# Other PSUM banks for the second tile's sequence product and the first pair, and matrix blocks and a transposition moved, in a four-layer attention and Fourier kernel

## The chip, the core and the metric

The kernel runs on one core of a Trainium2 chip. The metric is the device time of one execution in microseconds (us); lower is better. Five engines work from instruction queues of their own: TensorE (PE) multiplies matrices, VectorE (DVE), ScalarE (ACT) and GpSimd (POOL) do elementwise work, SyncE (SP) issues nearly all of the DMA transfers. PE writes its products to PSUM, which the kernel uses as eight banks of 128 x 512 fp32.

## The reference

Four sublayers follow each other, A, B, A, B, each with a residual around it, on x of 2048 rows by 640 columns:

```python
x = x + A(layernorm(x))      # layer 0;  layer 2 again, with the same weights
x = x + B(layernorm(x))      # layer 1;  layer 3 again

def A(x, wqkv, wo):          # 32 heads of 20; 8 keys per row at distances 0, 2, ..., 14
    q, k, v = split_heads(x @ wqkv)
    kg, vg = k[idx], v[idx]                    # idx = pos - 2 * arange(8), masked below 0
    attn = softmax(einsum("hsd,hswd->hsw", q, kg) * 20 ** -0.5)
    return einsum("hsw,hswd->hsd", attn, vg) @ wo

def B(x, Cr, Ci, Wr, Wi):    # real part of a two-dimensional Fourier transform
    a, b = x @ Wr.T, x @ Wi.T
    return Cr @ a - Ci @ b
```

Cr and Ci are 2048 x 2048, Wr and Wi 640 x 640, and they come as inputs, as do wqkv and wo.

## The kernel before

**Numbers.** Every fp32 operand of a product is split into a hi and a lo part in the type fp32r, and each product runs as three passes (hi by hi, hi by lo, lo by hi). A split is two instructions: ACT copies the hi part, and DVE (sometimes POOL) subtracts it to get the lo part. Both stand ahead of every product.

**Rows.** The 2048 rows are held in 4 chunks c of 4 blocks j of 128 rows, in a permuted order (even rows first), so that the dilated window becomes a plain one.

**Layer A** (`layer_a`, L242) is one plan written by hand. `at(step, phase, fn)` (L264) puts a function under a step, from -7 to 66, and a phase; at the end all steps are run through, and in each the phases in the order of the list PHASES (L827). All five engines keep exactly that order (`manual_schedule`, L831). In a step stand the product for q, k and v (`qkv_mm`, L352, into banks m0 and m1), the attention itself on DVE and POOL (`qk_mul` L428 with L431 and L433, `soft`, `soft_exp` with L447 and L460, `av_mul` L467 with L469 and then L484 to L486 on POOL), the transpositions (`pc_pe`, L327; L331 is ACT's copy of one), the product with wo (`wo_mm`, L509) and its addition to x (`wo_add`, L159), and the loads: L417 loads a window of k and v.

**Layer B** (`LayerB`, L865) has eight column tiles t of 256 output columns of the sequence transform, Cr and Ci side by side in 512 columns. Its work is in three parts:

- *z[0]*, the sequence product of tile 0: 16 steps s, each with the five 128-column pieces k of the normalised x against one block of cs (the matrix of Cr and Ci), 15 matmuls a step, added up in five banks. It is computed within the plan of the layer A before it, one third of a step at a time (table ZTHIRDS), by `z_mm` (L944, matmul L955). The blocks come in two ways. In layer 0, `c_load` loads the raw block to a buffer stg, `c_hi` (L915) and `c_lo` (L942) split it. In layer 2, `c_get` (L933) loads a block that was stored split in the DRAM buffer c0b. Into which of the buffers s0, s2, s3 a block goes is said by `c_tag` (L903), and s0 is also used by the last transpositions of the attention before `wo_mm`.
- *the first two tiles* (`run`, L1266): the five banks of z[0] are evacuated to SBUF as hi and lo (`evac`; the hi copies on ACT, the lo on DVE in L1012 and L1015), the matrices of the hidden transform are loaded and split (`load_w`; ACT L126, DVE L128 and L130; five blocks of wre and five of wim), then the 16 steps of z[1] follow (`zpart`), with the output product of tile 0's first half (`ymm`, matmul L1033, read out with L1046 of `yout`) after step 3 and the first 2 of 5 blocks of its second half after step 13. Beside them DVE, ACT and SP make 20 combinations of x for the pairs (`x_whole` L1078; `x_combine`: L1086, L1087, L1088 and the store L1089, through a ring of two stg buffers). At the end the rest of the output product and the evacuation of z[1].
- *the pairs* (`pair`, L1130): six tiles in three pairs, each with seven products m1 to m7 in Strassen's manner instead of eight. A pair first computes m5, m4 and m7 together in a loop of eight steps i, in two banks each (`product`, L1122). Raw blocks of cs come through `s_raw` (L1105) into buffers win (five) or xa (two), combinations of them are made by L1151, splits by ACT L1115 and DVE L1116, combinations of x are loaded by L1095.

The pair that ends layer 1 is called from `early` (L573) of layer 2 and runs with hooks: at some of its places, the first chunk of layer 2's x is normalised and transposed (`xt(j, part)`: the PE transposition L225 into the bank pq, ACT's L232 and DVE's L236).

**What sets the order.** In layer B only PE keeps the written order (`manual_schedule` of the tensor engine alone, in `run` and `pair`). The order on DVE, ACT, POOL and SP is chosen by the framework's scheduler when the program is built; on the chip each engine then works its list in order. A PSUM bank can be taken by a new product when the last reader of the old one is done. The banks before, in the places around the change:

```python
ZTAGS = ("m0", "m1", "xt", "t0", "t1")                                                   # z[0] and z[1]
            self.ym = [pt([P, 512], f"aux{e}") for e in range(2)]                            # ymm
                m5, m4, m7 = banks("m0", "m1"), banks("xt", "t0"), banks("t1", "pq")           # every pair
```

Of the kernel before, what the change touches and what calls it, by code (L numbers as in the profile page):

```python
# [26 lines left out]
P = 128  # L27
NC = 4
NJ = 4
# [23 lines left out]
STG = (-1, "dma2")  # L53
NWIN = 5
ZTAGS = ("m0", "m1", "xt", "t0", "t1")
NT = 8
NP = 8
NPAIR = 3
# [16 lines left out]
def tile_layers(ctx: ExitStack, tc: tile.TileContext, x, wqkv, wo, cs, wre, wim, out):  # L75
# [10 lines left out]
    def nm(base):  # L86
        uid[0] += 1
        return f"{base}_{uid[0]}"
# [4 lines left out]
    def pt(shape, tag, bufs=1):  # L93
        return ps.tile(shape, F32, tag=tag, name=nm(tag), bufs=bufs)
# [117 lines left out]
    def a_weights_q(q):  # L212
        wt = T([P, 2, KD, 3 * F], f"r1_{q}", F32R)
        for k in range(KD):
            split(wt[:, 0, k], wt[:, 1, k], wq_load1(q, k))
        return wt
# [25 lines left out]
    def layer_a(li, stats, handoff, prev):  # L242
# [21 lines left out]
        def at(step, phase, fn, *args):  # L264
            plan.setdefault((step, phase), []).append((fn, args))
# [5 lines left out]
        def x_load(c, j, tag="xa"):  # L271
            xnT[(c, j)] = load_x(xin[c], j, tag)
# [9 lines left out]
        def x_norm(c, j, fast=False):  # L282
            stats[c].apply(j, xnT[(c, j)], fast)

        def xt_pe(c, j, part, bank):
            if part == 0:
                xnT[(c, j, 1)] = T([P, 2, KD, P], f"s{j}", F32R)
            xnT[(c, j, "p", part)] = t_pe(xnT[(c, j)], part, bank)

        def xt_hi(c, j, part):  # L290
            t_hi(xnT[(c, j, 1)], part, xnT[(c, j, "p", part)])

        def xt_lo(c, j, part):
            t_lo(xnT[(c, j, 1)], part, xnT[(c, j, "p", part)])
# [278 lines left out]
        def early():  # L573
            def x_get(j):
                x_load(0, j)
                x_norm(0, j)

            def w0():
                with tc.issue_after(prev.dma.ins):
                    wq[0] = a_weights_q(0)  # L580

            def xt(j, part):
                xt_pe(0, j, part, "pq")
                xt_hi(0, j, part)
                xt_lo(0, j, part)

            prev.pair(
                NPAIR - 1,
                stats,
                {  # L590
                    2: lambda: (x_get(0), x_get(1)),
                    4: lambda: xt(0, 0),
                    5: lambda: (xt(0, 1), x_get(2)),
                    6: lambda: xt(1, 0),
                    7: lambda: (w0(), xt(1, 1), x_get(3)),
                    ("y", 1): lambda: xt(2, 0),
                    ("y", 2): lambda: xt(2, 1),
                    "end": lambda: (xt(3, 0), xt(3, 1)),
                },
            )  # L600
            for q in range(1, NQ):
                wq[q] = a_weights_q(q)
# [63 lines left out]
        if not first:  # L666
            early()
        pq = pt([P, 512], "pq")
# [47 lines left out]
        for u in range(NG):  # L716
# [9 lines left out]
            for jp in range(2):  # L726
                s = 2 * u + jp
# [21 lines left out]
        for c in range(2):  # L749
# [10 lines left out]
            for j in range(NJ):  # L760
                t = LNS[ly][c] + (2 - c) * j
# [35 lines left out]
        if prev is not None:  # L797
            for j2 in range(2):
                at(j2 - 3, "pe3", prev.ymm, NT - 1, j2, 0, KD)
                at(j2 - 2, "actl", prev.yout, NT - 1, j2, stats)  # L800
        last = 66
# [6 lines left out]
        for z in range(len(thirds) // 3):  # L808
            t = thirds[3 * z]
            if first and z in PRE:  # L810
                at(max(thirds[3 * z - 7] + 1, t - 3), "dmac", handoff.c_get, z)
            elif first:
                at(t - 2, "dmac", handoff.c_load, z)
                at(t - 1, "hi", handoff.c_hi, z)
                at(t - 1, "misc", handoff.c_lo, z, z < NJ)
            else:
                at(t - 1, "dmac", handoff.c_get, z)
            for p in range(3):
                at(thirds[3 * z + p], "pe3", handoff.z_mm, z, p)
        if first:  # L820
# [44 lines left out]
    class LayerB:  # L865
# [35 lines left out]
            nc.vector.tensor_scalar(self.xl[(c, j)], xr[(c, j)], nmean, rstd, op0=ALU.add, op1=ALU.mult)  # L901

        def c_tag(self, s, t=0):  # L903
            tags = ("s3", "s0", "s2") if self.li == 1 else ("s0", "s2", "s3")
            if t:
                return (tags[0], tags[-1 if self.li == 3 else 1])[s % 2]
            return tags[s % 3] if s < NST - 1 else "s1"

        def c_load(self, s, t=0):
# [33 lines left out]

        def z_mm(self, s, p, t=0):  # L944
            if s == 0 and p in (None, 0):
                self.z[t] = [pt([P, 512], tag) for tag in ZTAGS]
            c, j = divmod(s, NJ)
            order = [(i, k) for i in range(3) for k in range(KD)]
            if s in (0, NST - 1):
                order = [(i, k) for k in range(KD) for i in range(3)]  # L950
            if p is not None:
                order = order[5 * p : 5 * p + 5]
            for i, k in order:
                a, b = PASSES[i]
                self.last = nc.tensor.matmul(  # L955
                    self.z[t][k],
                    self.xn[c][:, a, j, k * P : (k + 1) * P],
                    self.ct[s][:, b],
                    start=s == 0 and i == 0,
                    stop=s == NST - 1 and i == 2,  # L960
                )
# [60 lines left out]
        def ymm(self, t, j2, k0, k1, emajor=False, ks=tuple(range(KD))):  # L1022
            zt = self.zt[t]
            if k0 == 0:
                self.ym = [pt([P, 512], f"aux{e}") for e in range(2)]
            order = [(k, e) for k in ks[k0:k1] for e in range(2)]
            if emajor:
                order.sort(key=lambda ke: ke[1])
            for k, e in order:
                for a, b in PASSES:  # L1030
                    for ri in range(2):
                        w = self.wr[:, b, k] if ri == 0 else self.wi[k][b]
                        self.last = nc.tensor.matmul(  # L1033
                            self.ym[e][:, :320],
                            zt[(k, a, ri)][:, j2 * P : (j2 + 1) * P],
                            w[:, e * 320 : (e + 1) * 320],
                            start=(k, a, b, ri) == (ks[0], 0, 0, 0),
                            stop=(k, a, b, ri) == (ks[-1], 1, 0, 1),
                        )
# [90 lines left out]
        def pair(self, p, nstats, hooks=None):  # L1130
            t1, t2 = 2 * p + 2, 2 * p + 3
# [4 lines left out]
            tags = wide  # L1136
# [30 lines left out]
            def banks(*tg):  # L1167
                return [pt([P, 512], x) for x in tg]
# [3 lines left out]
                    hooks[at]()  # L1172

            with tc.manual_schedule(engines={nc.tensor.engine}):
                m5, m4, m7 = banks("m0", "m1"), banks("xt", "t0"), banks("t1", "pq")
                for i in range(NP):
                    ends = i == 0, i == NP - 1
                    b22, b21, b11 = raw(t2, NP + i), raw(t1, NP + i), raw(t1, i)
# [17 lines left out]
                m1, m2 = banks("m0", "m1"), banks("xt", "t0")  # L1196
# [33 lines left out]
                for i in range(NP):  # L1230
                    ends = i == 0, i == NP - 1
                    if hooks is not None and i == 3:
                        tags = narrow
# [58 lines left out]
    st0 = [None] * NC  # L1292
    b1, b2 = LayerB(1), LayerB(3)
    layer_a(0, st0, b1, None)
    st2 = [None] * NC
    b1.run(st2)
    layer_a(2, st2, b2, b1)
    b2.run(None)
    b2.ytile(NT - 1, 0, None)
    b2.y_final(NT - 1)  # L1300

# [54 lines left out]
```

## Time and profile before

| | |
|---|---|
| timed, median of 3 runs | 1798.74 us (1796.4 to 1799.93) |
| the profiled execution | 1789.91 us |
| its span, first to last instruction | 1788.0 us |
| mean granted clock of PE | 0.994 |
| PE busy in L1033 (output products) | 226.4 us with r2a, 208.2 us with pr |
| PE busy in L362 (q, k, v) | 436.5 us |
| DVE in L1151, win<-win,win | 75.7 us busy, 45.7 us idle just before, most of it waiting for DMA |
| DMA | 425.15 MB, 238 GB/s in the mean |

The profile is one execution. Times in it are us from the span's start. "Busy" is the share of the span in which an engine has an instruction running; "idle before" is the time that it stood just ahead of an instruction, with the work that released it. A group's line names the line of the program, engine, operation, and out<-in buffers by their names without numbers. The layers follow each other in the span: layer 0 to about 380 us, layer 1's own part to about 870, layer 2 to about 1265, then layer 3. Layer 1 and layer 3 run the same code.

### The profile page before, as it was taken

To read this page: it belongs to the slowest core of one execution; us is meant where nothing else is said; L and a number is where in the kernel's file an instruction comes from. 1 tells how busy PE (TensorE), PEld (TensorE's weight loads), DVE (VectorE), ACT (ScalarE), POOL (GpSimd) and SP (SyncE) were. 2 spreads that over 40 slices of the span, in tenths; PEclk is the share of its full clock that TensorE was granted. 3 is DMA by queue.
4 is the path that set the end of the run, shared out by engine and by line. 5 is a ranking of instruction groups with operands and counts; after the bars stand their busy time and mean duration, and the time that the engine had idled before them with its cause. 6 is when DMAs were issued, how large, how long until landed. Compare 5 with 4: busy or idle time off the path is not lost.

```text
span 1788.0 us, 26460 instructions
## 1 busy us (share of the span) xinstructions
PE 1741.6 (97%) x8798; PEld 1507.1 (84%) x8798; DVE 1381.9 (77%) x2139; ACT 813.1 (45%) x1690; POOL 634.8 (36%) x593
## 2 busy tenths in 40 slices
PE   9999998989999999999999999999999999999999
PEld 7889887778888888888888889878787888888888
DVE  6999998887767767767738999989777677677673
ACT  4664544454445445445623344444534443443441
POOL 4899999940000000000017998889300000000000
PEclk9999999999999999999999999999999999999999
DMA  7896678758778687777737866687687766876761
GB/s 248 286 313 211 203 210 269 252 183 282 268 255 264 239 274 252 240 267 249 225 125 224 265 213 218 208 293 248 228 295 259 261 223 224 267 230 228 253 208 52
DMA packets 271849, 425.15 MB, mean 238 GB/s; under 512 B 22592, under 2 KB 150592, under 8 KB 271456
## 3 DMA queue, kind: packets, MB, share of 16 engines
q1 hardware_dynamic: 268512, 421.49, 71.6%
q10 hardware_dynamic: 3200, 1.97, 0.4%
q8 instruction: 70, 1.15, 0.3%
q14 instruction: 67, 0.55, 0.1%
HBM read 338.23 MB, written 85.14 MB: 237 GB/s over the span
## 4 chain that ended last, share of the span: by engine, by line
PE 62%; DVE 14%; POOL 12%; DMA 7%; issue 3%; ACT 2%; SPq 0%; DVEq 0%; ACTq 0%; POOLq 0%
PE aux L1033 13%; PE m L362 12%; PE m L1122 9%; PE t L1122 9%; PE pq L1122 5%; PE xt L1122 5%; POOL pr L484 4%; DVE pr L431 3%; POOL pr L433 3%; DMA win<-cs_in 2%; DVE pr L469 2%; POOL pr L485 2%; PE m L955 2%; PE aux L509 2%; PE t L955 2%
## 5 line engine op out<-in xcount | busy, mean ns | idle before, releaser
L362 PE MATMUL m<-r,s 128*128 128x480 f32 x1920 | 436.5, 382 | 2.1 <-ACT s L232 1.6
L362 PEld LDWEIGHTS m<-r,s 128*128 128x128 f32 x1920 | 355.2, 188 | 55.8 <-ACT s L232 2.6
L1115 ACT CAST r<-win 128x512 fp32r<-128x512 f32 x248 | 151.1, 620 | 172.6 <-DVE win L1151 81.1
L174 POOL TENSOR_TENSOR stats<-stats,mhalf 128x1 f32<-128x1 f32 (+1 forms) x40 | 29.8, 746 | 558.4 <-ACT stats L170 549.1
L1033 PE MATMUL aux<-r2a,zo 128*128 128x320 f32 x768 | 226.4, 309 | 0.0
L484 POOL TENSOR_TENSOR pr<-pr 128x640 f32<-128x640 f32 x126 | 205.9, 1634 | 33.8 <-DVE pr L469 33.2
L1033 PE MATMUL aux<-pr,zo 128*128 128x320 f32 x704 | 208.2, 308 | 0.0
L431 DVE TENSOR_TENSOR pr<-pq,win 128x1280 f32<-128x1280 f32 x128 | 189.8, 1483 | 16.4 <-ACT pq L404 12.3
L1116 DVE TENSOR_TENSOR r<-win,r 128x512 fp32r<-128x512 f32 x248 | 167.4, 688 | 45.0 <-ACT r L1115 43.5
L469 DVE TENSOR_TENSOR pr<-pq,win 128x1280 f32<-128x1280 f32 x128 | 190.9, 1491 | 4.3
L433 POOL TENSOR_TENSOR pr<-pr 128x640 f32<-128x640 f32 x128 | 183.3, 1432 | 16.5 <-DVE pr L431 16.3
L1122 PE MATMUL m<-r,r 128*128 128x512 f32 x606 | 156.4, 392 | 0.8 <-DVE r L1116 0.8
L1033 PEld LDWEIGHTS aux<-r2a,zo 128*128 128x128 f32 x768 | 144.1, 188 | 2.0
L1122 PEld LDWEIGHTS m<-r,r 128*128 128x128 f32 x606 | 113.5, 188 | 26.6 <-DVE r L1116 1.5
L1033 PEld LDWEIGHTS aux<-pr,zo 128*128 128x128 f32 x704 | 132.2, 188 | 2.1
L955 PE MATMUL m<-s,r 128*128 128x512 f32 x384 | 120.1, 400 | 13.4 <-POOL s L942 4.9
L1122 PE MATMUL t<-r,r 128*128 128x512 f32 x483 | 130.7, 393 | 2.0 <-issue 1.2
L955 PE MATMUL t<-s,r 128*128 128x512 f32 x384 | 119.1, 398 | 2.3 <-DVE ot L1015 1.5
L439 DVE TENSOR_REDUCE lg<-pr 128x64 f32<-128x640 f32 x128 | 103.9, 812 | 18.2 <-POOL pr L433 17.8
L485 POOL TENSOR_TENSOR pr<-pr 128x320 f32<-128x320 f32 x126 | 113.0, 897 | 9.9
L1151 DVE TENSOR_TENSOR win<-win,win 128x512 f32<-128x512 f32 x110 | 75.7, 690 | 45.7 <-DMA win<-cs_in 43.9
L1122 PEld LDWEIGHTS t<-r,r 128*128 128x128 f32 x483 | 90.5, 188 | 23.4 <-issue 1.6
(285 smaller groups left out, 3227.8 us busy)
## 6 DMA issues: line engine op xcount, KB each, us to landing
win<-cs_in SPq DMA_DIRECT2D x354, 256.0 KB, 4.2
r<-xc SPq DMA_DIRECT2D x240, 256.0 KB, 4.4
win<-kvb SPq DMA_DIRECT2D x96, 440.0 KB, 4.3
xa<-cs_in SPq DMA_DIRECT2D x122, 256.0 KB, 4.2
win<-kvb SPq DMA_DIRECT2D x64, 360.0 KB, 5.3
xc<-stg SPq DMA_DIRECT2D x40, 512.0 KB, 3.4
kvb<-stg SPq DMA_DIRECT2D x60, 320.0 KB, 4.7
xr<-xs SPq DMA_DIRECT2D x41, 320.0 KB, 3.6
```

What stands on the lines that cost most here:

```text
L362: nc.tensor.matmul(mt[g][:, : 3 * F], st[:, a, k], wq[q][:, b, k], start=n == 0, stop=n == 14)
L431: nc.vector.tensor_tensor(pr, q, wview(u, jp, 0, [[1, FE]]), op=ALU.mult)
L433: nc.gpsimd.tensor_tensor(pv[:, :, 0:10], pv[:, :, 0:10], pv[:, :, 10:20], op=ALU.add)
L439: nc.vector.tensor_reduce(lgs[u][:, 2 * jp : 2 * jp + 2].rearrange("p j w h -> p (j w h)"), prq.pop((u, jp))[:, :, 0:10], axis=AX.X, op=AL ...
L469: nc.vector.tensor_tensor(pr.rearrange("p j w (h d) -> p j w h d", d=DH), lgs[u][:, 2 * jp : 2 * jp + 2].unsqueeze(4).to_broadcast([P, 2, ...
L484: g.tensor_tensor(pr[:, :, 0:4], pr[:, :, 0:4], pr[:, :, 4:8], op=ALU.add)
L485: g.tensor_tensor(pr[:, :, 0:2], pr[:, :, 0:2], pr[:, :, 2:4], op=ALU.add)
L955: self.last = nc.tensor.matmul(self.z[t][k], self.xn[c][:, a, j, k * P : (k + 1) * P], self.ct[s][:, b], start=s == 0 and i == 0, stop=s = ...
L1033: self.last = nc.tensor.matmul(self.ym[e][:, :320], zt[(k, a, ri)][:, j2 * P : (j2 + 1) * P], w[:, e * 320 : (e + 1) * 320], start=(k, a, ...
L1115: nc.scalar.copy(hi, raw)
L1116: nc.vector.tensor_tensor(lo, raw, hi.bitcast(F32), op=ALU.subtract)
L1122: nc.tensor.matmul(bank, w(a, kb), hl[b], start=start and (a, b) == (0, 0), stop=stop and (a, b) == (1, 0),)
```

## The change

Six edits, with the same matmuls before and after:

- z[1] takes the banks aux0, aux1, pq, m0 and m1 (ZTAGS1); z[0] keeps its own.
- The two output products of tile 0 take the banks xt and t0; all others keep aux0 and aux1.
- The first pair's m5, m4 and m7 take t1 and pq, m0 and m1, xt and t0; the other pairs keep theirs.
- In layer 0's plan the lo parts of cs blocks 11 and 12 are computed on POOL and not on DVE.
- In layer 2's plan blocks 0 and 1 are loaded one step earlier (steps 48 and 49 instead of 49 and 50; block 2 stays at 50), and the buffers of layer 3's z[0] go round in the order s2, s0, s3 instead of s0, s2, s3. (The rewritten line for t=1 gives the same buffers as before.)
- In the pair with hooks, the last two transpositions come after blocks k=3 and k=4 of the output product, and not both at its end.

```diff
+ZTAGS1 = ("aux0", "aux1", "pq", "m0", "m1")
...
-                    "end": lambda: (xt(3, 0), xt(3, 1)),
+                    ("y", 3): lambda: xt(3, 0),
+                    ("y", 4): lambda: xt(3, 1),
...
-                at(t - 1, "misc", handoff.c_lo, z, z < NJ)
+                at(t - 1, "misc", handoff.c_lo, z, z < NJ or z in (11, 12))
             else:
-                at(t - 1, "dmac", handoff.c_get, z)
+                at(min(t - 1, 48 + z) if z < 3 else t - 1, "dmac", handoff.c_get, z)
...
         def c_tag(self, s, t=0):
-            tags = ("s3", "s0", "s2") if self.li == 1 else ("s0", "s2", "s3")
             if t:
-                return (tags[0], tags[-1 if self.li == 3 else 1])[s % 2]
+                return (("s3", "s0") if self.li == 1 else ("s0", "s3"))[s % 2]
+            tags = ("s3", "s0", "s2") if self.li == 1 else ("s2", "s0", "s3")
             return tags[s % 3] if s < NST - 1 else "s1"
...
-                self.z[t] = [pt([P, 512], tag) for tag in ZTAGS]
+                self.z[t] = [pt([P, 512], tag) for tag in (ZTAGS, ZTAGS1)[t]]
...
-                self.ym = [pt([P, 512], f"aux{e}") for e in range(2)]
+                self.ym = [pt([P, 512], tag) for tag in (("aux0", "aux1") if t else ("xt", "t0"))]
...
-                m5, m4, m7 = banks("m0", "m1"), banks("xt", "t0"), banks("t1", "pq")
+                if p == 0:
+                    m5, m4, m7 = banks("t1", "pq"), banks("m0", "m1"), banks("xt", "t0")
+                else:
+                    m5, m4, m7 = banks("m0", "m1"), banks("xt", "t0"), banks("t1", "pq")
```

When the changed program is built, the number of instructions of each engine stays, but for two that go from DVE to POOL. The scheduler's order changes at some places of layers 1 and 3. On PE the first three matmuls of m5 stand inside z[1]'s steps 12 and 13. On DVE, some of the splits L942 stand ahead of the L1088 that they were behind, and around the evacuation of z[1] the end of the list is, by lines:

```text
before: L1015 zo, L1046, L1046, L1015 ot, L1151 win<-xa, L1012 ot
after:  L1015 zo, L1151 win<-xa, L1046, L1046, L1015 ot, L1012 ot
```

In layer 2, SP's load of block 0 stands behind the store of L523 and ahead of two window loads; the load of block 1 stands where that of block 0 stood.

## The prediction

> **What bounds the kernel now.** I read the page first, then the waits of TensorE (PE), then its timeline around each place that the change touches, then the other engines' timelines there.
>
> ```profile
> span 1788.0 us, 26460 instructions
> PE 1741.6 (97%) x8798; PEld 1507.1 (84%) x8798; DVE 1381.9 (77%) x2139; ACT 813.1 (45%) x1690; POOL 634.8 (36%) x593
> PE 62%; DVE 14%; POOL 12%; DMA 7%; issue 3%; ACT 2%; SPq 0%; DVEq 0%; ACTq 0%; POOLq 0%
> ```
>
> PE is busy for 97% of the span, and no edit takes a matmul away. So a gain can only be a PE wait that goes, and a loss one that comes. A wait is counted if nothing later absorbs it: in the pairs PE runs through, so a delay there moves the end one to one; inside the attention layers PE waits for the other engines anyway.
>
> Waiting costs twice. Granted clock by window (start:end, length, busy us of PE, PEld, DVE, ACT, POOL with counts, clock, DMA share, GB/s):
>
> ```profile
> 356.50:360.00 3.50, 3.44 (x13) 3.44 (x14) 3.50 (x6) 0.11 (x1) 2.96 (x3) 0.53 0.67 200
> 1176.00:1182.00 6.00, 5.53 (x13) 4.37 (x14) 5.03 (x8) 1.58 (x6) 5.84 (x6) 0.50 1.01 319
> ```
>
> Each follows a wait of 2.10 and 2.07 us. The clock falls to half behind waits of about 2 us, on a grid of 3.41 us (half-clock stretches begin at 264.2, 295.0, 301.8, 356.4 and 1175.6). The same 30 matmuls of L509 took 6.12 us at 356.56 and 4.66 at 1243.54: one fall cost 1.46 us.
>
> **First edit: the banks (layers 1 and 3).** Before, the second tile's sequence product waits for the evacuation of the first tile's last banks. In layer 1 the trace has .24, .76 and .40 us at 401.04, 403.43 and 404.76; with the restart of the pipeline 1.89 us, in layer 3 1.96. With aux0, aux1, pq, m0 and m1 this goes. But the first output product (L1033) follows after four steps, and its k=4 terms need wim's fifth block:
>
> ```profile
> 422.70 0.83 DVE L128 SCALAR_TENSOR_TENSOR zo<-xa,zo 128x640 fp32r<-128x640 f32 x1 [1.01 <-ACT zo L126]
> ```
>
> That ends at 423.53 and PE reaches its terms at 423.58 already, so 1.0 of the 1.9 is lost again; .9 stays.
>
> What decides is the next place, the start of the first pair. There PE waits today for bank t1, freed by the last evacuation, L1012 (start, us, engine, line, operation, tiles, idle before and its releaser):
>
> ```profile
> 473.94 0.38 SPq L1105 DMA_DIRECT2D xa<-cs_in  x1
> ...
> 475.04 0.88 DVE L1046 TENSOR_TENSOR xr<-aux,xr 128x320 f32<-128x320 f32 x2
> 475.84 0.41 DVE L1015 TENSOR_TENSOR ot<-t,zo 128x256 fp32r<-128x256 f32 x1
> 477.57 0.69 DVE L1151 TENSOR_TENSOR win<-xa,win 128x512 f32<-128x512 f32 x1 [1.32 <-DMA xa<-cs_in]
> 478.18 0.68 DVE L1012 TENSOR_TENSOR ot<-t,ot 128x512 fp32r<-128x512 f32 x1
> ...
> 478.96 0.94 PE L1122 MATMUL t<-r,r 128*128 128x512 f32 x3 [0.80 <-PE t L1122]
> ```
>
> DVE works in program order: L1012 was behind L1151, which waited for a load of cs_in. PE had m5 and m4 (12 matmuls) to do meanwhile, and only m7 stood. The instruction order of the changed program puts L1151 further forward, ahead of both L1046 and of the L1015 for ot; and m4, not m7, now takes the banks that these free (m0 holds k=3, m1 k=4). From the landing at 477.57: L1151 .69, two L1046 .88, L1015 .41 with small overlaps end at 479.45, L1012 at 480.1. m4's three matmuls on m0 start at about 479.6, those on m1 at 480.3, and m7 at 481.1 instead of 478.96: **+2.1 us**. The load hangs on the 20 combinations (L1086 to L1089) ahead on DVE and its ring of two buffers, not on PE, so the .9 won before only lengthens this wait. Layer 3 has the same order:
>
> ```profile
> 1364.14 0.69 DVE L1151 TENSOR_TENSOR win<-xa,win 128x512 f32<-128x512 f32 x1 [0.94 <-DMA xa<-cs_in]
> ...
> 1365.53 0.94 PE L1122 MATMUL t<-r,r 128*128 128x512 f32 x3 [1.16 <-issue]
> ```
>
> By the same sum m0 is free at 1366.0 and m7 starts at 1367.5: **+2.0**. Bounds for each: 1.5 and 4, since the load's landing isn't fixed (L1088 now follows L1086 at once and stands for ACT, .7 us; the same kind of load takes 3.0 us at 1361.16 and 3.6 at 473.94).
>
> PE then stands from about 475.6 to 479.6, and from 1362.0 to 1366.1: 4 us each. By the rows above the clock falls behind each: 1.46 and, as part of the window may lie in the wait, 1.4 taken, **+2.8** for both (0 to 2 × 1.7, half of a 3.41 us window). [...]
>
> Other effects of the banks: the first output product's banks xt and t0 are read out by 512 at the latest, and the next product that wants them starts behind 518: nothing.
>
> **Second edit: the lo parts of blocks 11 and 12 move to POOL (end of layer 0).**
>
> ```profile
> 356.83 1.44 DVE L942 TENSOR_TENSOR s<-stg,s 128x512 fp32r<-128x512 f32 x1
> ...
> 364.22 1.28 DVE L942 TENSOR_TENSOR s<-stg,s 128x512 fp32r<-128x512 f32 x1
> 281.60 1.27 POOL L942 TENSOR_TENSOR s<-stg,s 128x512 fp32r<-128x512 f32 x1
> ```
>
> DVE loses 1.44 and 1.28, POOL gains about 1.27 twice (bounds .68, DVE's undisturbed row, and 1.94, POOL's slowest there) against 4.1 us of its idle between 354 and 382. The first removal is hidden: DVE waits for a load of x at 363.39 anyway. The second moves DVE's last product, which ends the layer at 382.2 with POOL's at 382.06. POOL's L174 comes .75 later and so PE's wait at 371.34, which the later ending hides. **−1.2** (0 to −1.8). The waits at 356.56 and the fall of the clock there stay: block 10 is still DVE's.
>
> **Third edit: matrix blocks 0 and 1 in layer 2.** Order and tags change together.
>
> ```profile
> 1166.47 0.92 SPq L417 DMA_DIRECT2D win<-kvb  x2
> 1173.10 0.32 SPq L933 DMA_DIRECT2D s<-c0b  x1
> 1177.32 1.97 SPq L933 DMA_DIRECT2D s<-c0b  x2
> ...
> 1176.47 2.92 PE L955 MATMUL m<-s,r 128*128 128x512 f32 x6 [2.07 <-DMA s<-c0b]
> ...
> 1190.71 0.37 ACT L331 CAST ot<-aux 128x256 fp32r<-128x256 f32 x1 [8.37 <-PE aux L327]
> ```
>
> Block 0's load stands on SP until its buffer s0 is free (1173.10), and the two behind it come at 1177.32, landing after 6.75. Block 0 now uses s2, free at about 1165, ahead of the two window loads: issued near 1166.5, it lands by 1173.2 even at 6.75 us. PE is ready at 1174.4. Block 1 issues at 1173.1 and lands 3.3 to 6.75 later, against 1177.9 when PE wants it. So the 2.07, the half clock and the 1.19 at 1184.12 go, and PE's transposition L327 comes 3.7 to 5.2 earlier. ACT (8.37) waits for it with an exponential behind, and so DVE's 1.51 at 1192.14. But what ends the layer is the attention's last product, at POOL 1266.69; POOL has 4.46 us idle between 1190 and 1202, hardly any after it to 1232, and the next window load limits DVE with 3.53 at 1189.14 while the DMA queues stand at a share of 1.0. I take **−2.5** between 0 and −4.5.
>
> **Fourth edit: the last transposition (start of layer 2).** PE waited 1.04 and .57 for ACT:
>
> ```profile
> 899.20 0.70 PE L362 MATMUL m<-r,s 128*128 128x480 f32 x2 [1.04 <-ACT s L232]
> ```
>
> With xt(3,0) and xt(3,1) between output products the first wait goes, 1.2 with its restart; some .3 may come back on bank pq, which the second part now wants sooner. **−.9** (−.3 to −1.9).
>
> **Sum.** −1.2 − .9 − 2.5 + 2.1 + 2.0 + 2.8 = +2.3. The profiled execution took 1789.91 (span 1788.0 and 1.91 around), so it would take 1792.2. The median of the timed runs is 1798.74, 8.8 above the profiled one; the difference carried over gives **1801.0**. A measurement of this kernel can tell about 0.2%, 3.6 us, from no change: "same" is 1795.1 to 1802.3.
>
> **Rivals.**
> Faster: the cs_in load that L1151 waits for lands earlier, because splits moved past the combinations fill DVE's idle and close the chain sooner. Each us takes one off both waits. From 1.5 us on (a PE wait of 2.5) the clock may hold too: +2.3 − 3.0 − 2.8 = −3.5, at 2 us −4.5, 1794.2; at 3.6 us both waits vanish, with today's .80 and 1.16 as well, and the z product's .9 is kept: 1790. For it: DVE idles .7 several times in the chain for ACT. Against: the chain's last steps follow DMA (L1086 waits for xc<-stg). Layer 2 paying in full (−4.5) would help this side. Chance .25.
> Slower: layer 2 pays nothing, since POOL's saturated stretch sets its end whatever PE does at 1184 (+2.5), and the load lands .7 later in both layers behind the delayed L1088 (+1.4): 1804.9; with full half-clock windows 1805.5. For it: POOL is busy 29.16 of 30 us in 1202 to 1232. Point of decision: whether POOL's 4.46 idle at 1190 shrinks. Chance .28.
> [...] Chance .10.
> Forecast: .37, own range 1798 to 1804, of it .25 within 0.2% and .12 above.
> That the change doesn't do what it says is excluded for the order: the new program's listing shows each move.
>
> **Chances.** Faster .25 + .02 = .27; same .25 + .08 = .33; slower .28 + .12 = .40. The range reaches from the partly earlier load with layer 2 in full (1792) to the slower rival with both loads 1.5 later (1807).
>
> **What would show it.** Right: DVE with an idle ahead of L1151 near 476 and behind it L1046, L1015, L1012; a PE wait of some 4 us just ahead of m4 and a clock near half behind it, in layers 1 and 3; no PE wait on ot tiles near 401 and 1286; SP's c0b load behind 1166; PE's L327 near 1185; PE's wait at 899 gone. Wrong: the pairs start without a wait above 2 us, or L1151 finds its data; POOL's idle at 1190 unchanged with the layer's end unmoved; a new wait of PE on pq near 898.

## The result, and the profile after

The changed kernel took 1801.13 us in the median (22 runs, 1795.26 to 1805.89), the kernel before, run beside it, 1796.3 (22 runs, 1790.2 to 1800.64). The ratio is 1.0028, with a 95% interval of 1.0018 to 1.0037: about 5 us slower. The prediction said +2.3 us and 1801.0; that the figure nearly meets the measured one is partly luck, since the kernel before came out at 1796.3 in 22 runs where it had 1798.74 in 3.

From here on, lines are those of the changed kernel where a fence is of it: L1124 is the pairs' product (L1122 before), L1153 the combination of raw blocks (L1151), L1014 and L1017 the evacuations (L1012, L1015), L1048 the read-out of the output product (L1046), L127 the hi copy (L126).

The page of the changed kernel, from its first lines:

```profile
span 1800.3 us, 26446 instructions
PE 1745.3 (97%) x8798; PEld 1511.1 (84%) x8798; DVE 1382.0 (77%) x2137; ACT 812.1 (45%) x1690; POOL 636.7 (35%) x595
...
PE 57%; DVE 16%; POOL 11%; DMA 9%; issue 3%; ACT 2%; SPq 0%; ACTq 0%; DVEq 0%; POOLq 0%
```

Busy times are within 2 us of those before, but for PE's and the weight loads', which are about 4 us longer: nine windows of 3.41 us at half clock lie in this span, six in the one before. On the chain, DVE and DMA have gained what PE lost. The two spans, 1788.0 and 1800.3, must not be subtracted: the first execution was among the quickest (1789.91, below all 22 timed ones), and a second profile of the kernel before took 1796.04.

PE's waits in the changed kernel, around the first two tiles of layer 1 (line, what it waited for: us in total, times, longest):

```profile
PE m L1124 <- DVE ot L1017: 2.8, 1, 2.8
PE xt L1035 <- ACT zo L127: 2.3, 1, 2.3
...
PE xt L1035 <- DVE zo L129: 0.7, 1, 0.7
```

and of layer 3:

```profile
PE xt L1035 <- ACT zo L127: 2.9, 1, 2.9
PE m L1124 <- DVE ot L1017: 2.5, 1, 2.5
```

The waits of z[1] for L1015 and L1012 are gone. In their place stand one in the first output product (L1035, at its k=4 terms, for the two parts of wim's fifth block) and one ahead of m4 (L1124). DVE and PE around the second, in the changed kernel:

```profile
474.56 0.42 DVE L1017 TENSOR_TENSOR zo<-m,zo 128x256 fp32r<-128x256 f32 x1
476.77 0.69 DVE L1153 TENSOR_TENSOR win<-xa,win 128x512 f32<-128x512 f32 x1 [1.79 <-DMA xa<-cs_in]
477.38 0.48 DVE L1048 TENSOR_TENSOR xr<-xt,xr 128x320 f32<-128x320 f32 x1
477.78 0.48 DVE L1048 TENSOR_TENSOR xr<-t,xr 128x320 f32<-128x320 f32 x1
478.18 0.42 DVE L1017 TENSOR_TENSOR ot<-m,zo 128x256 fp32r<-128x256 f32 x1
478.51 0.68 DVE L1014 TENSOR_TENSOR ot<-m,ot 128x512 fp32r<-128x512 f32 x1
...
478.74 2.90 PE L1124 MATMUL m<-r 128*128 128x512 f32 x6 [2.80 <-DVE ot L1017]
481.44 1.18 PE L1124 MATMUL xt<-r,r 128*128 128x512 f32 x3
```

This shows the queue: L1153 stands 1.79 us for its load, and behind it, in order, the read-outs and the L1017 that frees m0. m4 starts 0.14 us after that L1017 ends, and its six matmuls take 2.90 us where six in a row take 1.56 (m7 in the run e6 below). Why so long is shown by the windows of 3.41 us (start:end, length, busy us of PE, PEld, DVE, ACT, POOL, clock, DMA share, GB/s):

```profile
475.30:478.72 3.42, 0.64 (x3) 0.20 (x2) 1.95 (x5) 1.61 (x3) 0.00 (x0) 1.00 0.38 125
478.72:482.13 3.41, 3.39 (x8) 2.73 (x9) 1.76 (x3) 1.78 (x5) 0.00 (x0) 0.50 0.41 131
...
905.38:908.79 3.41, 1.75 (x10) 1.32 (x9) 1.45 (x4) 2.38 (x7) 0.00 (x0) 1.00 0.25 96
908.79:912.20 3.41, 3.41 (x21) 3.13 (x20) 0.00 (x0) 0.56 (x1) 0.00 (x0) 1.00 0.02 5
...
1373.01:1376.42 3.41, 1.27 (x6) 1.08 (x7) 3.20 (x7) 0.34 (x1) 0.00 (x0) 1.00 0.51 173
1376.42:1379.84 3.42, 3.42 (x10) 2.65 (x9) 1.20 (x2) 0.88 (x2) 0.00 (x0) 0.50 0.43 107
```

Behind a window with 0.64 or 1.27 us of PE work the next has a clock of 0.50; behind one with 1.75 it has 1.00.

### The profile page after: what moved, and what is told of

Read it like the earlier page. It is cut to its first block, busy times and chain, and to the rows that moved or that the text cites. A ratio compares the mean times of both kernels' runs of the same rounds, so it can differ in the third digit from the quotient of the medians.

```text
span 1800.3 us, 26446 instructions
## 1 busy us (share of the span) xinstructions
PE 1745.3 (97%) x8798; PEld 1511.1 (84%) x8798; DVE 1382.0 (77%) x2137; ACT 812.1 (45%) x1690; POOL 636.7 (35%) x595
## 4 chain that ended last, share of the span: by engine, by line
PE 57%; DVE 16%; POOL 11%; DMA 9%; issue 3%; ACT 2%; SPq 0%; ACTq 0%; DVEq 0%; POOLq 0%
PE aux L1035 11%; PE m L363 11%; PE m L1124 9%; PE t L1124 9%; PE pq L1124 5%; PE xt L1124 5%; DVE pr L432 3%; POOL pr L485 3%; DVE pr L470 3%; POOL pr L434 3%; DMA win<-cs_in 2%; POOL pr L486 2%; DMA xc<-stg 2%; PE aux L510 1%; DVE lg L440 1%
## 5 line engine op out<-in xcount | busy, mean ns | idle before, releaser
L363 PE MATMUL m<-r,s 128*128 128x480 f32 x1920 | 436.3, 382 | 4.3 <-ACT s L233 3.9
L363 PEld LDWEIGHTS m<-r,s 128*128 128x128 f32 x1920 | 355.3, 188 | 57.8 <-ACT s L233 4.7
L1035 PE MATMUL aux<-r2a,zo 128*128 128x320 f32 x672 | 198.2, 310 | 0.0
L1035 PE MATMUL aux<-pr,zo 128*128 128x320 f32 x616 | 182.2, 308 | 0.0
L1124 PE MATMUL t<-r,r 128*128 128x512 f32 x519 | 142.6, 397 | 0.0
L1124 PE MATMUL m<-r,r 128*128 128x512 f32 x534 | 137.8, 392 | 0.7 <-DVE r L1118 0.7
L1035 PEld LDWEIGHTS aux<-r2a,zo 128*128 128x128 f32 x672 | 126.1, 188 | 1.7
L1124 PEld LDWEIGHTS m<-r,r 128*128 128x128 f32 x534 | 100.4, 188 | 23.5 <-DVE r L1118 1.0
L1124 PEld LDWEIGHTS t<-r,r 128*128 128x128 f32 x519 | 99.1, 191 | 23.0
L1035 PEld LDWEIGHTS aux<-pr,zo 128*128 128x128 f32 x616 | 115.6, 188 | 1.9
L370 ACT COPY stg<-m 128x480 f32<-128x480 f32 x128 | 70.9, 554 | 81.8 <-PE m L363 61.7
L1153 DVE TENSOR_TENSOR win<-win,win 128x512 f32<-128x512 f32 x110 | 75.7, 690 | 39.1 <-DMA win<-cs_in 37.4
```

The lines of the kernel that those rows point to most:

```text
L363: nc.tensor.matmul(mt[g][:, : 3 * F], st[:, a, k], wq[q][:, b, k], start=n == 0, stop=n == 14)
L1035: self.last = nc.tensor.matmul(self.ym[e][:, :320], zt[(k, a, ri)][:, j2 * P : (j2 + 1) * P], w[:, e * 320 : (e + 1) * 320], start=(k, a, ...
L1124: nc.tensor.matmul(bank, w(a, kb), hl[b], start=start and (a, b) == (0, 0), stop=stop and (a, b) == (1, 0),)
```

## The experiments

Every run was profiled, and eleven were timed beside the kernel before. Since one execution differs from the next by some us in the pairs' waits for loads, three measures from the trace are set beside the time. *Stage*: PE's time from the start of the last product with wo of layer 0 (layer 2) to the start of the 36th matmul of the first pair, the stretch of the bank edits. *Evacuated*: when the last evacuation of z[1] ends on DVE (L1012 before, L1014 after), counted from the stage's start. *Lag*: from the end of DVE's last combination (L1088 before, L1090 after) to the first matmul of m7. "Step 4" is the first output product behind step 4 of z[1] instead of 3, "swap" is m4 on xt and t0 and m7 on m0 and m1.

| kernel | ratio to before (95%) | stage, layer 1 / 3 | evacuated, layer 1 / 3 | lag, layer 1 / 3 |
|---|---|---|---|---|
| before | 1 | 94.8 / 96.5 | 89.3 / 91.0 | 7.4 / 6.4 |
| before, profiled again (c1) | | 96.3 / 97.7 | 90.8 / 92.1 | 6.9 / 7.1 |
| changed | 1.0028 (1.0018 to 1.0037) | 99.7 / 102.7 | 91.8 / 94.8 | 11.4 / 9.7 |
| banks alone (e1) | 1.0043 (1.0028 to 1.0058) | 101.9 / 99.3 | 94.1 / 91.3 | 11.5 / 9.9 |
| transposition alone (e2) | 0.9994 (0.9981 to 1.0007) | 97.3 / 97.8 | 91.8 / 92.3 | 7.0 / 6.6 |
| blocks alone (e3) | 0.9986 (0.9972 to 0.9999) | 95.8 / 97.8 | 90.3 / 92.2 | 7.1 / 6.6 |
| changed, step 4 (e4) | 0.9991 (0.9976 to 1.0006) | 96.5 / 94.4 | 88.6 / 88.0 | 4.9 / 4.3 |
| changed, load in win (e5) | 1.0046 (1.0028 to 1.0065) | 102.9 / 100.3 | 95.2 / 92.4 | 11.5 / 10.5 |
| step 4 and swap (e6) | 0.9963 (0.9947 to 0.9979) | 95.4 / 94.8 | 90.1 / 89.2 | 2.6 / 3.5 |
| old banks, step 4, blocks (e7) | 0.9976 (0.9960 to 0.9991) | 95.5 / 96.9 | 89.9 / 91.3 | 4.2 / 5.8 |
| e6, transposition back (e8) | 0.9968 (0.9956 to 0.9980) | 96.4 / 97.2 | 89.6 / 90.5 | 3.2 / 4.6 |
| changed, swap (e9) | 1.0012 (1.0002 to 1.0022) | 100.9 / 100.3 | 93.8 / 94.7 | 10.2 / 8.8 |
| e6, block 2 earlier (e10) | 0.9944 (0.9932 to 0.9956) | 97.2 / 95.1 | 90.6 / 89.5 | 3.8 / 3.5 |
| e6 again (e11) | 0.9972 (0.9957 to 0.9987) | 96.8 / 97.0 | 90.0 / 89.9 | 3.8 / 4.1 |

**Which part loses (e1, e2, e3).** The parts of the diff, one at a time: e1 has ZTAGS1 and the banks of `ymm` and `pair`, e2 only the hooks, e3 the two lines of the plan and `c_tag`.

> Only the bank edits (z[1] on aux0, aux1, pq, m0, m1; tile 0's output products on xt, t0; the first pair's banks). Theory 1: they are the loss. They move PE's wait from the start of z[1] to the k=4 terms of the first output product (in the changed kernel 2.34 and 0.71 us at 421, 2.92 at 1315) and to m4 at the first pair (2.80 and 2.45 us, where 0.80 and 1.16 stood), each with a half-clock window behind some of them: 4 to 10 us slower than before, ratio 1.002 to 1.006, all four waits in the trace. Theory 2: the banks are neutral and the loss lies in the other edits: within 2 us of before.

> Only the last transposition's two parts between the output products. The prediction had 0.9 us faster. Theory 1 (from the trace of the changed kernel, where PE waits 2.20 and 1.66 us for ACT's L233 at 900 and 908 instead of 1.04 and 0.57): the transposition comes too early for ACT, whose queue stands behind weight loads, so 1 to 2.5 us slower, with those waits in the trace. Theory 2: these waits came only because the stretch was entered at another time: 0 to 1 us faster, waits as before or smaller.

> Only the matrix blocks: lo parts 11 and 12 on POOL in layer 0, and the earlier loads with the other buffer order in layer 2. Theory 1: 1 to 4 us faster; the end of layer 0 comes 1 to 2.5 us earlier, and in layer 2 the 2.07 us wait for block 0 goes, but a wait of 2 to 3.5 us for block 2 comes, with the DMA queues full, so that PE's L328 (L327 before) comes only 1 to 2 us earlier. Theory 2 (the prediction's terms in full): 3.7 us faster, L328 4 to 5 us earlier in its stretch, no wait above 1 us for a block.

The banks lose 7.7 us (1.0043), the blocks gain 2.5, the transposition changes nothing that can be told. The three ratios multiply to 1.0023, beside 1.0028 for all together. Theory 1 holds for e1 (though at 1314 the wait was 1.18 and 0.71 us) and for e3. For e2 its waits are there, but not its loss in time: 1.1 us faster, with an interval from 3.4 us faster to 1.3 us slower. The same place in e2, and below it in the repeated profile of the kernel before:

```profile
894.25 0.49 PE L225 MATMUL pq<-ident,xa 128*128 128x128 f32 x3
898.22 2.46 PE L362 MATMUL m<-r,s 128*128 128x480 f32 x10 [1.73 <-ACT s L232]
...
905.75 3.11 PE L362 MATMUL m<-r,s 128*128 128x480 f32 x13 [1.66 <-ACT s L232]
```

```profile
894.04 0.49 PE L225 MATMUL pq<-ident,xa 128*128 128x128 f32 x3
897.88 1.70 PE L362 MATMUL m<-r,s 128*128 128x480 f32 x7
...
902.30 0.71 PE L362 MATMUL m<-r,s 128*128 128x480 f32 x2 [1.20 <-ACT s L232]
...
903.91 3.10 PE L362 MATMUL m<-r,s 128*128 128x480 f32 x13 [0.57 <-ACT s L232]
```

Behind the transposition at 894 both start the next product near 898. Before, PE used the time for 24 output matmuls; now only 12 stand there, and PE waits 1.73 us for ACT's copy of block 2. The wait of 1.20 was moved forward, not taken away, and the last one grew.

**What makes the banks lose (e4, e5, e9).** e4 changes one number of the changed kernel:

```diff
-                    if s == 3:
+                    if s == 4:
                         self.ymm(0, 0, 0, KD)
```

The scheduler's order on DVE then has L1153 behind the last evacuation.

> The changed kernel with tile 0's first output product behind step 4 of z[1] instead of step 3. In its program order DVE's L1153 that waits for the load of cs_in stands behind the last evacuations. Theory 1: both new waits go: none above 0.5 us at the k=4 terms near 425 and 1315, none above 1 us ahead of m4 near 478 and 1370; 6 to 12 us faster than the changed kernel, 2 to 6 us faster than before. Theory 2 (the waits come from the banks, not from the order on DVE and the time of wim): the wait ahead of m4 stays at 2 us or more, and the time within 2 us of the changed kernel.

By the ratios it is 6.6 us faster than the changed kernel, and about level with the kernel before, where theory 1 had 2 to 6 us faster; the waits at the k=4 terms are gone, the one ahead of m4 is smaller but still above the 1 us expected, and the six matmuls behind it take 2.90 us, as in the changed kernel, where the clock was 0.50. PE in e4:

```profile
473.06 0.97 PE L1124 MATMUL pq<-r,r 128*128 128x512 f32 x3 [1.13 <-DVE zo L1014]
475.82 2.90 PE L1124 MATMUL m<-r 128*128 128x512 f32 x6 [1.78 <-DVE ot L1017]
478.52 1.15 PE L1124 MATMUL xt<-r,r 128*128 128x512 f32 x3
```

The lag fell by more than the wait, from 11.4 to 4.9, but it can't be compared between the two orders. DVE in e4:

```profile
472.33 0.68 DVE L1014 TENSOR_TENSOR zo<-pq,zo 128x512 fp32r<-128x512 f32 x1
472.93 0.68 DVE L1090 TENSOR_TENSOR stg<-stg 128x512 fp32r<-128x512 f32 x1
...
475.59 0.68 DVE L1014 TENSOR_TENSOR ot<-m,ot 128x512 fp32r<-128x512 f32 x1
...
477.99 0.69 DVE L1153 TENSOR_TENSOR win<-xa,win 128x512 f32<-128x512 f32 x1 [0.40 <-DMA xa<-cs_in]
```

The L1153 that waits for the load is now last. But the last combination (L1090) has also moved, behind a part of the evacuations, and ends 86.0 us into the stage in place of 82.7; that shortens the lag by itself. The end of the evacuations is the fairer measure: 88.6 and 88.0 us into the stage, where the changed kernel has 91.8 and 94.8. What is left ahead of it is DVE's work (combinations, splits and evacuations without a gap from 467 on), and PE comes early to it. e4 moves two things at once, the output product on PE and the order on DVE. The wait ahead of m4 is tied to the order by its trace; how the 6.6 us divide between that wait and the vanished k=4 waits is open, since no run has the one change without the other.

e5 gives the load another ring:

```diff
-            tags = wide
+            tags = wide if p else (("win", NWIN), ("xa", 2)) + (("win", NWIN),) * 5
```

> The changed kernel, with the first pair's loads of cs_in after the first two in the ring of five win buffers and none in the ring of two xa (the order of all engines' work as in the changed kernel, the DVE instruction that waits for the load still ahead of the evacuations). Theory 1: the wait ahead of m4 has the price of that load's late buffer; if the load can be issued earlier, DVE's wait ahead of L1153 falls from 1.8 to under 1 us and PE's ahead of m4 from 2.8 and 2.45 to under 2, and the half-clock window behind it may go: 2 to 6 us faster than the changed kernel. Theory 2: the evacuations are late by DVE's own work ahead of them, not by the load: PE's wait stays above 2 us in both layers and the time within 2 us of the changed kernel.

This told nothing of the price of the load. The ring of win was no sooner free: SP and DVE in e5 show

```profile
475.22 1.71 SPq L1107 DMA_DIRECT2D win<-cs_in  x3
...
480.13 0.69 DVE L1153 TENSOR_TENSOR win<-win,win 128x512 f32<-128x512 f32 x1 [1.96 <-DMA win<-cs_in]
```

The load of that L1153 is one of the three at 475.22, 87.9 us into the stage or later; in the changed kernel it was issued at 86.0. PE waited 3.24 and 2.51 us ahead of m4, the lag stayed at 11.5, and the time was no shorter (1.0046). The order on DVE, the same as in the changed kernel, goes with the same lag.

e9 keeps that order and step 3, and lets m4 and m7 change places:

```diff
-                    m5, m4, m7 = banks("t1", "pq"), banks("m0", "m1"), banks("xt", "t0")
+                    m5, m4, m7 = banks("t1", "pq"), banks("xt", "t0"), banks("m0", "m1")
```

> The changed kernel, its output product behind step 3 as it was, only with m4 on xt and t0 and m7 on m0 and m1. DVE's order keeps L1153, which waits for the load, ahead of the evacuations. Theory 1 (the place of that wait on DVE and the k=4 wait are the loss, and the banks alone mend little): PE's wait ahead of m4 falls by 0.6 to 1 us in each layer, the k=4 waits of 2 to 3 us stay: 0 to 4 us faster than the changed kernel, not faster than before. Theory 2 (which of the two products takes m0 and m1 is all): as fast as e6, 5 us under the kernel before.

```profile
480.31 1.15 PE L1124 MATMUL xt<-r 128*128 128x512 f32 x3 [2.42 <-DVE xr L1048]
481.26 1.48 PE L1124 MATMUL t<-r 128*128 128x512 f32 x3
```

Theory 1, though the wait fell less than it had: 2.42 and 1.72 us in place of 2.80 and 2.45. It is now for L1048, which also stands behind L1153; the lag falls by 1.1 and 0.9 us, and the kernel is some 3 us faster than the changed one by the ratios, still not faster than before.

**Better versions (e6, e7, e8, e10, e11).** e6 has both edits, step 4 and the swap; e11 is e6 once more.

> The changed kernel with the output product behind step 4, and in the first pair m4 on xt and t0 and m7 on m0 and m1 (instead of the other way round). In the run with step 4 alone PE waited 1.78 and 1.18 us ahead of m4 for the L1017 that frees m0. Theory 1: xt and t0 are free about 1 us earlier, by the two L1048, so the wait falls to 0.5 to 1 us and m7 finds its banks free: 1 to 3 us faster than step 4 alone. Theory 2: DVE sets the pace of this stretch whatever banks are taken: no wait less, the same time within 1.5 us.

> The run e6 again, beside the three others on their chip: 1788 to 1793 us, ratio to the kernel before 0.995 to 0.998, with PE's waits at the first pair under 1 us ahead of m4 and none of 2 us at the k=4 terms.

PE in e6:

```profile
474.99 0.96 PE L1124 MATMUL pq<-r,r 128*128 128x512 f32 x3 [2.09 <-DVE zo L1014]
476.59 0.96 PE L1124 MATMUL xt<-r 128*128 128x512 f32 x3 [0.64 <-DVE xr L1048]
477.39 0.89 PE L1124 MATMUL t<-r 128*128 128x512 f32 x3
478.11 1.56 PE L1124 MATMUL m<-r,r 128*128 128x512 f32 x6
```

Theory 1, with ratios of 0.9963 and 0.9972, some 5 and 3 us under e4 where 1 to 3 were expected: m7 finds its banks free. Now the wait stands ahead of m5's second bank, for the third evacuation. The lag is the shortest, but the stage tells how little of the gain over the kernel before lies here: in the four kernels with both edits (e6, e8, e10, e11) it took 96.5 and 96.0 us in the mean, in the four with the old banks and order (before, c1, e2, e3) 96.1 and 97.4. By the stages, most of the gain is the blocks' (−0.8 and −2.7 us, below).

e7 is the kernel before with `if s == 4` and the edits of e3.

> The kernel before with its own banks, the output product behind step 4, and the matrix block edits (lo parts on POOL, earlier loads). L1151 stands behind the last evacuation in its program order. Theory 1 (what counts is the place of the load's wait on DVE, not the banks): PE's waits at the start of z[1] stay (1.9 us in sum), those ahead of m7 (0.80 and 1.16) fall under 0.5: 3 to 6 us faster than before, at least as fast as the changed kernel with step 4. Theory 2 (the new banks carry the gain of the run with step 4): 1 to 3 us slower than the run with step 4 and the new banks.

At 0.9976 it is 4 us faster than before, as theory 1 has it, and no slower than e4; 2.5 of the 4 are the blocks' (e3). m7's wait is gone in layer 1 and stayed at 1.20 in layer 3, which theory 1 did not have. The trace shows why: in layer 3 of e7, L1151 still stands ahead of the last evacuation:

```profile
1365.13 0.69 DVE L1151 TENSOR_TENSOR win<-xa,win 128x512 f32<-128x512 f32 x1 [1.06 <-DMA xa<-cs_in]
1365.74 0.68 DVE L1012 TENSOR_TENSOR ot<-t,ot 128x512 fp32r<-128x512 f32 x1
```

So the wait follows the place of L1151 here too, with the old banks. They do nearly as well as the new ones even so. Whether the 1 to 2 us between e7 and e6 are real, the intervals leave open. e8 puts both parts of the transposition back to "end":

> The run e6 (step 4, m4 on xt and t0, m7 on m0 and m1) with both parts of the last transposition at the end again. Theory 1 (the earlier transposition costs: PE waited 2.71 and 1.66 us for ACT's L233 at 896 and 903 in e6, 1.20 and 0.57 in the repeated run of the kernel before): 1 to 3 us faster than e6, with waits like those of the kernel before. Theory 2 (as measured alone, no difference that can be told): within 1.5 us of e6.

Theory 2: 0.9968 beside 0.9972 for e11. e10 loads block 2 of layer 2 a step earlier as well:

```diff
-                at(min(t - 1, 48 + z) if z < 3 else t - 1, "dmac", handoff.c_get, z)
+                at(min(t - 1, 48 + min(z, 1)) if z < 3 else t - 1, "dmac", handoff.c_get, z)
```

> The run e6 with the load of block 2 in layer 2 one step earlier as well. Theory 1 (the block waits in layer 2 are a matter of the full DMA queues at 1176 to 1190): the block lands earlier, PE's wait of 1.5 to 3.3 us for it shrinks below 1, but the window loads behind it land later and DVE's wait ahead of L432 grows; the layer's end and the time within 1.5 us of e6. Theory 2: the wait goes and the time with it, 1.5 to 4 us faster than e6.

In the changed kernel block 2 comes late: SP's loads of the blocks, and PE, in its layer 2:

```profile
1173.46 0.38 SPq L935 DMA_DIRECT2D s<-c0b  x1
...
1180.06 0.32 SPq L935 DMA_DIRECT2D s<-c0b  x1
...
1184.23 0.91 SPq L935 DMA_DIRECT2D s<-c0b  x1
...
1191.70 0.90 PE L957 MATMUL m<-s,r 128*128 128x512 f32 x2 [3.33 <-DMA s<-c0b]
```

and in e10 SP, and DVE's wait for the window:

```profile
1175.36 0.80 SPq L935 DMA_DIRECT2D s<-c0b  x2
...
1189.75 1.49 DVE L432 TENSOR_TENSOR pr<-pq,win 128x1280 f32<-128x1280 f32 x1 [1.75 <-DMA win<-kvb]
```

PE's wait for a block is gone, and DVE's wait for the window, 1.75, did not grow (2.16 in e11, 0.56 in e6); by the time theory 2. It is the fastest version, 1787.82 us in the median of 5, ratio 0.9944 to the kernel before; its stretch of layer 2, from the 61st matmul of L363 to the last one of L510, took 357.7 us, where the nine other profiles with the block edits have 358.4 to 361.4.

The kernel before was profiled again:

> The kernel before, profiled once more: its first profiled execution, 1789.91 us, is below all but the fastest of its timed runs. Expected 1794 to 1800 us, with the differences to the first profile in the pairs' waits for loads and in half-clock windows, and the same waits at 401 to 405, 479 and 1365 as in the first.

It took 1796.04 us with the expected waits; m7 of layer 3 starts 6.4 us later than in the first profile, out of small differences in the stages before.

## Why the prediction was right, and where not

- **The wait ahead of m4.** Right in place, cause and order, instruction by instruction, and in the two half-clock windows at 478.72 and 1376.42. Its length was not: 2.80 and 2.45 us in place of 4 each. PE came to m4 88.6 and 91.9 us into the stage (forecast, from its own times: 86.0 and 87.5), since it had lost more in the output product, and m0 came free 1.3 and 2.7 us later than forecast. The sum had +2.1 and +2.0 for the wait and 1.4 each for the clock, 3.5 and 3.4 us a layer. The stage means of the four kernels with these banks and this order (changed, e1, e5, e9), less those of the four with the old ones (before, c1, e2, e3), give 101.3 − 96.1 = 5.2 and 100.7 − 97.4 = 3.2; e1's time has 7.7 for both. The sum of 6.9 was somewhat small, and the part that was small is the clock: PE's waits in the stage add up to 6.3 and 5.1 us in the mean of the first four and to 3.1 and 4.5 in the others, which is +3.8 beside the forecast's +4.1, and 4.6 of the 8.4 are left for the clock, beside 2.8. The forecast counted one half-clock window in each layer. The eight stages of the first four kernels hold fourteen, seven behind the wait ahead of m4 and seven behind the k=4 waits; those of the others hold none. Less PE's waits, a stage takes 93.0 us in the mean of the others, and in the first four about 1.3 more for each window that it holds.
- **"1.0 of the 1.9 is lost again."** Mis-sized: the first output product took 12.5 and 13.9 us in place of 9.0, so the k=4 terms lost 3.4 us in layer 1 (2.34 and 0.71 idle, and the first matmul behind each took 0.41 us in place of 0.31) and 4.9 in layer 3 (2.92 idle, and behind it two windows at a clock of 0.50, in which such matmuls took 0.47 us or 0.64 in place of 0.31). The hi copy L127 that I took to depend on its load also stands behind a copy for a combination on ACT:

```profile
419.36 0.69 DVE L1088 TENSOR_TENSOR stg<-s 128x512 f32<-128x512 f32 x1 [2.43 <-DMA xc<-stg]
...
420.13 0.62 ACT L1089 CAST stg<-stg 128x512 fp32r<-128x512 f32 x1 [4.65 <-DVE stg L1088]
420.65 0.73 ACT L127 ACTIVATE zo<-xa 128x640 fp32r<-128x640 f32 x1
...
421.44 0.41 PE L1035 MATMUL xt<-zo,ot 128*128 128x320 f32 x1 [2.34 <-ACT zo L127]
```

  The forecast held that what PE wins or loses before m4 only changes how long it waits there, since DVE's combinations do not hang on PE. That fits while the clock holds, and less well when it falls. Among the eight stages with these waits, the 20 combinations took 67.1 and 66.5 us in the two without a half-clock window behind the k=4 waits (the changed kernel's layer 1, e1's layer 3), and 68.3 to 70.6 in the six with one or two; the stages took 99.7 and 99.3, and 100.3 to 102.9. The changed kernel's layer 3 shows how PE's delay comes to DVE, through the buffers of the split blocks that z[1] frees late:

```profile
1323.95 0.62 ACT L917 CAST s<-win 128x512 fp32r<-128x512 f32 x1 [2.86 <-PE m L957]
1324.60 0.70 DVE L944 TENSOR_TENSOR s<-win,s 128x512 fp32r<-128x512 f32 x1 [2.79 <-ACT s L917]
```

  How much of the difference is this, eight stages can't say: in the old order, without such waits, the combinations took 67.0 to 69.5.
- **Other effects of the banks.** "Nothing" was right: PE has no wait from 485 to 545 in the changed kernel. But the times given there, 512 and 518, are those of the first pair's own products on xt and t0, not of the first output product.
- **POOL instead of DVE at the end of layer 0.** Predicted −1.2. Layer 0's last product with wo comes at 388.0 us in the mean of the ten profiles with the edit, at 388.8 in the four without: −0.8, of the size expected, though single profiles with it lie between 387.4 and 389.9.
- **Blocks in layer 2.** Predicted −2.5. The stretch of layer 2 took 359.9 in the mean of nine profiles with it, 362.6 in the four without: −2.7. Right as a sum; but I let block 2's wait of 1.19 vanish with the others, where 1.5 to 3.3 us of wait stayed in the nine (3.0 to 3.9 in the other three profiles without the edit), and e10 shows that another step would have removed it.
- **The transposition.** The step that failed: "the first wait goes". It came earlier instead, as 1.73 us in e2 and 2.20 in the changed kernel, and for ACT's copy, not for the bank pq that the prediction had named as a risk. Predicted −0.9; from the last pair product of layer 1 to that 61st matmul the eight profiles with the edit took 38.5 us in the mean, the six without 38.0 (single ones from 36.2 to 39.9), and e2's time leaves room for −0.9 as for +0.5. I had seen that the transpositions go between the output products, but did not ask what the 24 matmuls had covered.
- **The sum.** With the stage means, −0.8 + 8.4 − 2.7 + 0.5 = +5.4, beside +5.0 measured and +2.3 predicted. Most of the difference is the banks' clock, and the transposition's 1.4, which is not clear of the scatter. So the total came near although several of its terms were mis-sized, in part by luck. The faster rival (an earlier load) did not happen: L1153 had its data 89.4 and 92.4 us into the stage, L1151 88.0 to 90.5 and 89.7 to 91.0 in the four profiles of the old order. The slower rival was at most half right: the load came later in layer 3, but layer 2 did pay.
- **The clock.** The fall behind both waits came: the windows that held most of them had 0.64 and 1.27 us of PE work, and the next ran at 0.50. For the chance of .10 no run shows a ground; what the runs showed is a fall behind seven of the eight waits ahead of m4 in the changed kernel, e1, e5 and e9.

What stays open: how much of the stages' spread is the half-clock windows behind the k=4 waits (the changed kernel's layer 3 had two at 1314.98 and took 102.7; three kernels with the same order had one or none there and took 99.3 to 100.3); and how much of e10's lead is the block, since its trace shows 2.2 us less in layer 2 than the nine's mean, but only 0.7 less than e6's, and the ratio is 5 us below that of e11.

## What to carry to other kernels

A wait that is taken from one place moves to the next one that the slower engine sets: here the stretch ends when DVE has done its combinations and evacuations, and PE arriving earlier only waits longer, and then runs at half clock for a window of 3.41 us (at 478.72 and 1376.42 of the changed kernel). Where a scheduler orders an engine's queue, look in the new program at what stands ahead of the instruction that frees a resource; here one step later for the output product, which moved such an instruction, was worth 6.6 us (changed to e4) and 7 to 9 (e9 to e11 and e6), the choice of banks for m4 and m7 3 to 5. Check a measure for what it starts from: the lag looked like a gain because its own start had moved. When an instruction is moved forward, list what had been working while its result was on the way.

## What the runs showed of the hardware

In the profile of the changed kernel the clock fell behind windows of 3.41 us that PE had worked in for 0.40, 0.64, 1.05, 1.27 and 1.34 us (at 1188.69, 475.30, 1311.57, 1373.01 and 867.84), and did not behind those with 1.76 and 1.75 (898.56 and 905.38). In that of the kernel before it fell behind windows with 1.48, 1.57 and 1.65 (352.98, 298.37 and 1172.18), and did not behind one with 1.79 (281.30). Single windows of other runs lie otherwise: no fall behind one with 1.51 (e1, 260.06), a fall behind 1.74 (e11, 1364.52) and 2.03 (e8, 379.67). The lengths of the waits order it less well: at the one of 2.07 us that ends at 1176.47 in the kernel before the clock fell (at 1175.60), at the one of 2.20 that ends at 900.21 in the changed kernel it did not. One half-clock window cost 1.34 us in m4's six matmuls (2.90 in place of 1.56); at its clock of 0.50 half of its 3.41, 1.7, is the most by this estimate, as much as many of the waits themselves.
